# Column-normalised attention and a top-1 mixture of experts on one core: each batch's mixing set beside the next batch's Gram matrix, sums moved from GpSimd to VectorE and TensorE, two float32 Gram matrices, twelve float32 expert blocks

## The chip, the core and the metric

The kernel runs on one core of a Trainium2 chip. Its engines work side by side, each through its own instructions in the order in which they were queued: TensorE (PE; its weight loads are PEld), VectorE (DVE), ScalarE (ACT), GpSimd (POOL) and SyncE (SP), which here only starts transfers. An engine whose next instruction has to wait starts nothing behind it. Transfers run on 16 DMA engines, started by SP (plain loads and stores) and by POOL (gathers and scatters with row numbers). The metric is device microseconds of one execution.

## The reference

```
qn = q / (norm(q, axis=1) + 1e-6);  kn = k / (norm(k, axis=1) + 1e-6)    # q, k, v: [4, 5056, 256]
s = kn.transpose(0, 2, 1) @ qn / tau;  a = softmax(s, -1)                # a: [4, 256, 256]
x = (v @ a).reshape(20224, 256)
logits = x @ w_gate;  e_idx = argmax(logits, 1);  probs = softmax(logits)
for e in range(8):                                                       # w1[e]: [256, 1024], w2[e]: [1024, 256]
    mask = e_idx == e
    out[mask] = probs[mask, e] * sigmoid(x[mask] @ w_output_gate[:, e]) * (relu(x[mask] @ w1[e]) @ w2[e])
```

## The kernel before

For each of the four batches there are three kinds of work, and a fourth for the whole.

**Gram** (`gram`, L244). 20 steps, each of two tiles of 128 rows of q and k (two transfers of 256 KB). TensorE adds k-transposed times q into `s_ps` (L282). Batch 0 multiplies in float32; batches 1 to 3 split q and k into a float32r high part (ACT, L265) and the remainder (DVE, L267) and multiply three times. The squares (ACT, L275) are summed into two accumulators `acc`, one on POOL and one on DVE (L277). At the end TensorE sums them over the rows (L294, L297), and some twenty small steps turn them into norms, softmax and the split matrix `ah`, `al` (L305 to L351).

**Mix** (`mix`, L356). 5 groups of 1024 rows of v: transposes (L378), a split (L382, L384), x and its logits in three multiplications (`x_ps`, L389 to L391), x stored to `xd` (L398). `route` (L404) finds each row's expert and place, and POOL scatters 8 x 128 entries into the table `tab` (L474).

**Checkpoints and blocks.** At a checkpoint (`checkpoint`, L601) the number of full blocks of 256 rows that each expert surely has is turned into a list of jobs (`table`, L491), after a mark is read back from `tab` (L486). There is one after group 2 of batch 0 and one at each batch's end. A block gathers row numbers (L686) and rows (L702), gets its expert's weights (L672), and goes through the two layers: `h_ps` (L790 to L792), ReLU and split (L794, L795), `y_ps` (L647 to L649), scaling (L653) and a scatter to the output (L655). The first 8 blocks are *cold*: float32 with the weights as they come (L772, L645), fetched anew for each block. The others are *hot*: float16 with high and low parts, three multiplications, and no fetch when the block two places earlier had the same expert. 72 full and 21 half blocks.

**Weight preparation** (`prep`, L212), 16 steps of 1 MB, two buffers. Load (L218, L222); sum of squares (ACT, L228); its sum over partitions by `partition_all_reduce` on POOL (L230); a power of two (DVE, L200 to L207); high part (ACT, L233); low part (DVE, L234); two stores to `wsc` (L238). Hot blocks need all 16.

The functions are generators. `_drive` (L28) emits from several side by side in proportion to their lengths, and a list scheduler then sets each engine's order from the dependencies, its own idea of durations and hints: `attend` (L862) ran Gram and mix of a batch one after the other with high priority, and `issue_after` held single transfers behind others.

Of the kernel before, what the change touches and what calls it, by code (L numbers as in the profile page):

```python
# [21 lines left out]
P = 128  # L22
# [18 lines left out]
def tile_colnorm_attention_then_top1_moe(  # L41
# [35 lines left out]
    CKS = [(0, 2), (0, NG - 1)] + [(b, NG - 1) for b in range(1, B)]  # L77
# [29 lines left out]
    WHOLE = (0,)  # L107
    NCOLD = 8
    GATE = 1
    HOLD = 3  # L110
    PGATE = 4
# [6 lines left out]
    first = []  # L118
# [6 lines left out]
    v_loads = [[] for _ in range(B)]  # L125
# [59 lines left out]
    def pow2(m, kk, scale, inv):  # L185
        """scale = 2^(kk - floor(log2 m)), inv = 1 / scale; both exact."""
# [10 lines left out]
    def root2(ss, kk, scale, inv):  # L197
        """scale: the power of two for which 2^(kk - 2) < scale * sqrt(ss) < 2^kk; inv = 1 / scale."""
# [13 lines left out]
    def prep():  # L212
        for e in range(E):
            for half in range(2):
                raw = big.tile([P, HW1], F32, tag="raw", name=f"raw{e}_{half}")
                with tc.issue_after(v_loads[0][PGATE]):
# [11 lines left out]
                nc.scalar.activation(hi, raw, AF.Square, accum_out=ss)  # L228
                tot = sm.tile([P, 1], F32, tag="wtot", name="wtot")
                nc.gpsimd.partition_all_reduce(tot, ss, P, bass_isa.ReduceOp.add)  # L230
# [11 lines left out]
    a_of = {}  # L242

    def gram(b):  # L244
        s_ps = ps_s.tile([P, CC, C], F32, tag="s", name=f"s_ps{b}")
        accs = [one.tile([P, 2, 2, C], F32, tag=f"acc{i}", name=f"acc{b}_{i}") for i in range(2)]
        nstep = NT // 2
        for st in range(nstep):
            t0 = 2 * st
            last = st == nstep - 1  # L250
            qk = ld.tile([P, 2, 2, C], F32, tag="qk", name=f"qk{b}_{st}", bufs=4)
            for i, src in enumerate((q, k)):
                main = src[b, :MAIN].rearrange("(p t) c -> p t c", p=P)
                nt = 1 if last else 2
                with tc.issue_after(v_loads[b - 1][GATE]) if b else nullcontext():
                    nc.sync.dma_start(qk[:, i, :nt, :], main[:, t0 : t0 + nt, :])
                    if last:
                        nc.sync.dma_start(qk[:REM, i, 1, :], src[b, MAIN:])
                if last and REM < P:
                    nc.gpsimd.memset(qk[REM:, i, 1, :], 0.0)  # L260
            if b in WHOLE:
                terms = [(qk, qk)]
            else:
                hi = wk.tile([P, 2, 2, C], F32R, tag="qkh", name=f"qkh{b}_{st}")
                nc.scalar.copy(hi, qk)  # L265
                lo = wk.tile([P, 2, 2, C], F32R, tag="qkl", name=f"qkl{b}_{st}")
                nc.vector.tensor_tensor(out=lo, in0=qk, in1=hi.bitcast(F32), op=ALU.subtract)  # L267
                terms = [(hi, hi), (hi, lo), (lo, hi)]
            on_pool = (st % 3 != 1) if b == 0 else (st % 2 == 0)
            acc = accs[int(on_pool)]  # L270
            if st < 2:
                nc.scalar.activation(acc, qk, AF.Square)
            else:
                sq = wk.tile([P, 2, 2, C], F32, tag="sq", name=f"sq{b}_{st}")
                nc.scalar.activation(sq, qk, AF.Square)  # L275
                eng = nc.gpsimd if on_pool else nc.vector
                eng.tensor_tensor(out=acc, in0=acc, in1=sq, op=ALU.add)  # L277
            for t in range(2):
                for c in range(CC):
                    cs = slice(c * P, (c + 1) * P)  # L280
                    for n, (kt, qt) in enumerate(terms):
                        nc.tensor.matmul(  # L282
                            s_ps[:, c, :], kt[:, 1, t, cs], qt[:, 0, t, :],
                            start=st == 0 and t == 0 and c == 0 and n == 0,
                            stop=last and t == 1 and n == len(terms) - 1,
                            skip_group_check=True,
                        )
            yield

        n_ps = ps_x.tile([P, 2, C], F32, tag="x", name=f"n_ps{b}")  # L290
        k_ps = ps_x.tile([P, 512], F32, tag="x", name=f"k_ps{b}")
        parts = [(i, t) for i in range(2) for t in range(2)]
        for n, (i, t) in enumerate(parts):
            nc.tensor.matmul(n_ps[:, 0, :], onesf, accs[i][:, 0, t, :], start=n == 0, stop=n == 3)  # L294
        for c in range(CC):
            for n, (i, t) in enumerate(parts):
                nc.tensor.matmul(  # L297
                    k_ps[:, c : c + 1], accs[i][:, 1, t, c * P : (c + 1) * P], onesf[:, 0:1],
                    start=n == 0, stop=n == 3, skip_group_check=True,
                )  # L300
        rq = one.tile([P, C], F32, tag="rq", name=f"rq{b}")
        rk = sm.tile([P, CC], F32, tag="rk", name=f"rk{b}")
        for r, ss in ((rq, n_ps[:, 0, :]), (rk, k_ps[:, :CC])):
            root = one.tile(list(r.shape), F32, tag="root", name="root", bufs=2)
            nc.scalar.activation(root, ss, AF.Sqrt)  # L305
            nc.vector.tensor_scalar(out=root, in0=root, scalar1=1e-30, scalar2=None, op0=ALU.max)
            nc.vector.reciprocal(r, root)
            nc.vector.tensor_tensor(out=r, in0=ss, in1=r, op=ALU.mult)
            nc.vector.tensor_tensor(out=r, in0=r, in1=root, op=ALU.add)
            nc.vector.tensor_scalar(out=r, in0=r, scalar1=0.5, scalar2=1e-6, op0=ALU.mult, op1=ALU.add)  # L310
        nc.vector.tensor_scalar(out=rk, in0=rk, scalar1=tau_b, scalar2=None, op0=ALU.mult)
        nc.vector.reciprocal(rq, rq)
        nc.vector.reciprocal(rk, rk)
# [14 lines left out]
        for c in range(CC):  # L328
            nc.vector.tensor_scalar(out=s[:, c, :], in0=s[:, c, :], scalar1=se[:, c : c + 1], scalar2=None, op0=ALU.mult)
# [18 lines left out]
        nc.scalar.copy(ah[:, :, :C], s)  # L348
        nc.scalar.copy(ah[:, :, C:], awv)
        nc.vector.tensor_tensor(out=al[:, :, :C], in0=s, in1=ah[:, :, :C].bitcast(F32), op=ALU.subtract)  # L350
        nc.vector.tensor_tensor(out=al[:, :, C:], in0=awv, in1=ah[:, :, C:].bitcast(F32), op=ALU.subtract)  # L351
# [4 lines left out]
    def mix(b):  # L356
        ah, al = a_of[b]
        for g in range(NG):
# [5 lines left out]
            for i in range(R // 2):  # L364
                if i % 2 == 0:
                    vt = ld.tile([P, 4, C], F32, tag="v", name=f"v{b}_{g}_{i}", bufs=3)
                    if np_ < P:
                        nc.gpsimd.memset(vt[np_ // 32 * 32 :], 0.0)
# [122 lines left out]
    def table(nm, mf, unit, Q, g0, step, nc_=0, wait=None):  # L491
# [81 lines left out]
        if nc_:  # L573
            nc.vector.tensor_copy(wi[:, :nc_], tmp[:, :nc_])
# [340 lines left out]
```

## Time and profile before

| | us |
|---|---|
| median of 3 runs | 1704.95 |
| lowest and highest run | 1701.8, 1712.46 |
| span of the profiled execution | 1590.9 |
| median less span | 114.05 |

The span runs from the first to the last instruction; what an execution takes around it the profile does not show. In a row of the timeline stand the start, the duration, the engine, the line, what is written from what, and in brackets the idle time before it and what ended that. "issue" in that place is time in which the engine waited for nothing that the profile shows. Lines such as L230 are those of the kernel before.

### The profile page before, as it was taken

The page shows a single profiled execution, that of the slowest core. Times are in us where ns is not written, and L with a number is a line of the kernel's source. Part 1 is how long each engine was busy: PE and PEld are TensorE (multiplying, and loading weights), DVE is VectorE, ACT ScalarE, POOL GpSimd, SP SyncE. Part 2 cuts the span into 40 slices and gives each one's busy share as a digit, 9 for nine tenths or more (in the row PEclk, how much of TensorE's full clock was granted, in tenths as well). Part 3 has the DMA queues.
Part 4 walks back from the last instruction along what each step waited for, and adds up shares of the span by engine and source line. Part 5 has one row for each costly group of instructions (what it writes and reads, how often), then busy time and mean ns, then how long its engine had stood idle before and what let it go on. Part 6 is the DMA issues. An engine that isn't in the chain of part 4 may idle for free. (4 is left out here: it accounts for less than half of the span.)

```text
span 1590.9 us, 28639 instructions
## 1 busy us (share of the span) xinstructions
PE 1320.8 (83%) x10982; PEld 1193.9 (75%) x10982; DVE 741.7 (47%) x1982; ACT 632.1 (40%) x1143; POOL 937.9 (59%) x860
## 2 busy tenths in 40 slices
PE   7585465576689578977999899999898999999998
PEld 6485455565679477876988788888787899889997
DVE  2674453341234467436456443443443454445543
ACT  3584453353355446433443232323232333333332
POOL 6344545454546457656567756556565677777774
PEclk9697768698789789998999999999999999999999
DMA  8388776464889477451433111111112535231120
GB/s 298 116 287 212 128 198 215 142 206 113 235 266 294 140 261 201 138 122 31 109 119 71 55 41 48 48 41 48 48 43 68 193 122 171 83 98 48 49 95 21
DMA packets 117565, 207.59 MB, mean 130 GB/s; under 512 B 40812, under 2 KB 70774, under 8 KB 111796
## 3 DMA queue, kind: packets, MB, share of 16 engines
q1 hardware_dynamic: 66420, 116.43, 26.0%
q0 software_dynamic: 51008, 89.33, 17.8%
q8 instruction: 86, 1.41, 0.4%
q14 instruction: 51, 0.42, 0.1%
HBM read 295.76 MB, written 60.59 MB: 224 GB/s over the span
## 5 line engine op out<-in xcount | busy, mean ns | idle before, releaser
L790 PE MATMUL h_ps<-xt,wbuf 128*128 128x256 f16 (+1 forms) x1360 | 343.4, 262 | 42.1 <-DVE hb L795 27.5
L794 ACT ACTIVATE hb<-h_ps 128x512 f16<-128x512 f32 (+1 forms) x340 | 185.1, 545 | 485.7 <-PE h_ps L792 485.4
L791 PE MATMUL h_ps<-xt,wbuf 128*128 128x256 f16 (+1 forms) x1360 | 343.7, 262 | 0.0
L792 PE MATMUL h_ps<-xt,wbuf 128*128 128x256 f16 (+1 forms) x1360 | 343.5, 262 | 0.0
L647 PE MATMUL y_ps<-wbuf,hb 128*128 128x256 f16 x1192 | 326.6, 274 | 2.6 <-DMA wbuf<-wsc,tb_wif 1.5
L649 PE MATMUL y_ps<-wbuf,hb 128*128 128x256 f16 x1192 | 326.4, 274 | 0.0
L648 PE MATMUL y_ps<-wbuf,hb 128*128 128x256 f16 x1192 | 326.4, 274 | 0.0
L795 DVE SCALAR_TENSOR_TENSOR hb<-h_ps,hb 128x512 f16<-128x512 f32 (+1 forms) x340 | 209.2, 620 | 166.3 <-ACT hb L794 163.2
L474 POOL DMA_INDIRECT tab<-r_ig,r_si x160 | 188.6, 1179 | 78.9 <-issue 39.1
L702 POOL DMA_INDIRECT xg<-xd,b_ig x165 | 176.4, 1069 | 94.3 <-issue 43.0
L655 POOL DMA_INDIRECT out_dram<-yo,b_ig x165 | 169.8, 1029 | 57.4 <-issue 36.8
L277 POOL TENSOR_TENSOR acc<-acc,sq 128x1024 f32<-128x1024 f32 x39 | 94.3, 2418 | 138.7 <-issue 70.5
L791 PEld LDWEIGHTS <-wbuf 128*128 128x128 f16 x1360 | 134.4, 99 | 39.7 <-issue 25.7
L672 POOL DMA_INDIRECT wbuf<-wsc,tb_wif x128 | 130.0, 1015 | 57.9 <-issue 26.4
L790 PEld LDWEIGHTS <-wbuf 128*128 128x128 f16 x1360 | 134.3, 99 | 36.3 <-DMA wbuf<-wsc,tb_wif 13.6
L728 DVE TENSOR_REDUCE b_mx<-xg 128x2 f32<-128x512 f32 (+1 forms) x85 | 52.7, 619 | 233.5 <-DMA xg<-xd,b_ig 233.5
L792 PEld LDWEIGHTS <-wbuf 128*128 128x128 f16 x1360 | 134.3, 99 | 13.2
L275 ACT ACTIVATE sq<-qk 128x1024 f32<-128x1024 f32 x72 | 75.8, 1060 | 144.6 <-POOL acc L277 94.2
L686 POOL DMA_INDIRECT b_ig<-tab,tb_gif x72 | 75.8, 1053 | 97.1 <-DMA out_dram<-yo,b_ig 69.1
L647 PEld LDWEIGHTS <-hb 128*128 128x128 f16 x1192 | 117.2, 98 | 15.4 <-DMA wbuf<-wsc,tb_wif 1.7
L648 PEld LDWEIGHTS <-hb 128*128 128x128 f16 x1192 | 117.3, 98 | 14.8 <-issue 1.3
L649 PEld LDWEIGHTS <-hb 128*128 128x128 f16 x1192 | 117.1, 98 | 14.3
(188 smaller groups left out, 2559.1 us busy)
## 6 DMA issues: line engine op xcount, KB each, us to landing
qk<-in_q_dram SPq DMA_DIRECT2D x76, 256.0 KB, 5.4
qk<-in_k_dram SPq DMA_DIRECT2D x76, 256.0 KB, 5.3
v<-in_v_dram SPq DMA_DIRECT2D x32, 512.0 KB, 7.5
raw<-in_moe_w_dram SPq DMA_DIRECT2D x16, 1024.0 KB, 13.4
xd<-st SPq DMA_DIRECT2D x16, 1024.0 KB, 8.3
wsc<-whi SPq DMA_DIRECT2D x16, 512.0 KB, 7.1
wsc<-raw SPq DMA_DIRECT2D x16, 512.0 KB, 9.4
v<-in_v_dram SPq DMA_DIRECT2D x8, 480.0 KB, 7.4
```

What stands on the lines that cost most here:

```text
L474: ins = nc.gpsimd.indirect_dma_start(out=tab[:, :], out_offset=bass.IndirectOffsetOnAxis(ap=si[:np_, t : t + 1], axis=0), in_=ig[:np_, t, ...
L647: nc.tensor.matmul(y_ps[:, t, :], hb[:, 0, f, tsl], w2s[:, 0, f, :], start=st, stop=False, **kw)
L648: nc.tensor.matmul(y_ps[:, t, :], hb[:, 0, f, tsl], w2s[:, 1, f, :], start=False, stop=False, **kw)
L649: nc.tensor.matmul(y_ps[:, t, :], hb[:, 1, f, tsl], w2s[:, 0, f, :], start=False, stop=fin, **kw)
L655: ins = nc.gpsimd.indirect_dma_start(out=out[:, :], out_offset=bass.IndirectOffsetOnAxis(ap=job["ig"][:, t, 0:1], axis=0), in_=yo[:, t, :] ...
L672: nc.gpsimd.indirect_dma_start(out=dst.bitcast(F32) if cold else dst, out_offset=None, in_=wraw[half] if cold else wsc[half][:, :], in_off ...
L702: ins = nc.gpsimd.indirect_dma_start(out=xg[:, g % XGB, t, :], out_offset=None, in_=xd[:lim, :], in_offset=bass.IndirectOffsetOnAxis(ap=jb ...
L790: nc.tensor.matmul(hp, w1s[:, 0, c, fs], xh, start=fi == 0 and c == 0, stop=False, **kw)
L791: nc.tensor.matmul(hp, w1s[:, 0, c, fs], xl, start=False, stop=False, **kw)
L792: nc.tensor.matmul(hp, w1s[:, 1, c, fs], xh, start=False, stop=fin, **kw)
L794: nc.scalar.activation(hh, h_ps[:, :, :w], AF.Relu)
L795: nc.vector.scalar_tensor_tensor(out=hb[:, 1, 2 * fp : 2 * fp + 2, :w], in0=h_ps[:, :, :w], scalar=0.0, in1=hh, op0=ALU.max, op1=ALU.subtract,
```

## The change

The emission: batch b's mix now runs beside batch b+1's Gram; with batch 1 also the weight preparation; blocks from batch 1 on. `attend`, its priority and most hints are gone, and the checkpoint within batch 0 too, so that the first list comes after the whole of batch 0.

```diff
-    for b in range(B):
-        par = [(mix(b) if b == 0 else attend(b), (NG * (R // 2 + 1) + (NT // 2 + 1) * (b > 0)) / FAST)]
-        n = sum(q for (cb, cg), q in quotas.items() if cb < b or (cb == b and cg < NG - 1)) - LAG - nout
...
+    for b in range(B):
+        par = [(mix(b), NG * (R // 2 + 1))]
+        if b < B - 1:
+            par.append((gram(b + 1), NT // 2 + 1))
+        n = sum(q for (cb, cg), q in quotas.items() if cb < b) - LAG - nout
+        if b == 1:
+            par.append((preps, 2 * E + 1))
+        if n > 0:
+            par.append((some(n * FC // 2), n * FC // 2))
...
-    CKS = [(0, 2), (0, NG - 1)] + [(b, NG - 1) for b in range(1, B)]
+    CKS = [(b, NG - 1) for b in range(B)]
...
-    WHOLE = (0,)
-    NCOLD = 8
+    TS = 4
+    WHOLE = (0, 1)
+    NCOLD = 12
```

The sums: the weights' sum over partitions becomes a TensorE product with ones; all squares are added on DVE into one `acc`; a Gram's sums are one column each for q and k, their roots are taken on [128, 4], and the q norms are spread by a product with a diagonal matrix. Three instructions that scaled or split `s` become part of the split.

```diff
+                w_ps = ps_x.tile([P, 512], F32, tag="x", name="w_ps")
+                nc.tensor.matmul(w_ps[:, 0:1], onesf, ss, start=True, stop=True)
                 tot = sm.tile([P, 1], F32, tag="wtot", name="wtot")
-                nc.gpsimd.partition_all_reduce(tot, ss, P, bass_isa.ReduceOp.add)
+                nc.vector.tensor_copy(tot, w_ps[:, 0:1])
...
-                eng = nc.gpsimd if on_pool else nc.vector
-                eng.tensor_tensor(out=acc, in0=acc, in1=sq, op=ALU.add)
+                    nc.vector.tensor_tensor(out=acc, in0=acc, in1=sq, op=ALU.add)
...
-            nc.tensor.matmul(n_ps[:, 0, :], onesf, accs[i][:, 0, t, :], start=n == 0, stop=n == 3)
+        for i in range(2):
+            for c in range(CC):
+                for t in range(2):
+                    nc.tensor.matmul(
+                        k_ps[:, i * CC + c : i * CC + c + 1], acc[:, i, t, c * P : (c + 1) * P], onesf[:, 0:1],
+                        start=t == 0, stop=t == 1, skip_group_check=True,
+                    )
...
+            nc.vector.tensor_scalar(out=dq[:, c, :], in0=ident, scalar1=r[:, c : c + 1], scalar2=None, op0=ALU.mult)
+        nc.tensor.matmul(n_ps[:, :C], onesf, dq.rearrange("p c m -> p (c m)"), start=True, stop=True)
```

q and k come in transfers of four tiles (512 KB each, three buffers in place of four half as large). Cold blocks, too, no longer fetch weights when the block two places earlier had the same expert. The rest of the diff follows from these.

What this does to each engine's order, at three places. POOL in the weight preparation of before: `ISA` rows load code, `wtot` is the sum over partitions, `acc` a Gram's sum, `tab` the scatter of routing.

```order
L230 ISA
L230 ISA wtot<-wss 128x1
L277 ISA
L277 TENSOR_TENSOR acc_1_3989<-acc_1_3989,sq_16_5448 128x1024
L702 DMA xg<-xd,b_ig 128x256 x2
L230 ISA
L230 ISA wtot<-wss 128x1
L672 DMA wbuf_160<-in_moe_w_dram,tb_wif_993 128x2048
```

The same sum now, on PE between a cold block's products (`h_ps`, `y_ps`) and mixing (`x_ps`):

```order
L760 MATMUL h_ps<-xt_1690,wbuf_160 128x256 x4
L635 MATMUL y_ps<-wbuf_161,hb_1651 128x256
L225 MATMUL w_ps<-wss,onesf 128x1
L388 MATMUL x_ps<-ah_1424,vh 128x272
L389 MATMUL x_ps<-al_1425,vh 128x272
```

The sum has left POOL, whose queue now holds transfers only, and PE waits for ACT's `wss` at that row.

PE early in the mixing of batch 0, before (`s_ps` is Gram 1 from split parts, `vt_ps` the transposes):

```order
L391 MATMUL x_ps<-ah_423,vl 128x272
L389 MATMUL x_ps<-ah_423,vh 128x272
L282 MATMUL s_ps_1431<-qkh_5_1685 128x256
L390 MATMUL x_ps<-al_424,vh 128x272
L378 MATMUL vt_ps<-ident,v_0_2_486 128x128 x4
L282 MATMUL s_ps_1431<-qkl_5_1687,qkh_5_1685 128x256
L282 MATMUL s_ps_1431<-qkh_5_1685,qkl_5_1687 128x256
```

and now:

```order
L390 MATMUL x_ps<-ah_385,vl 128x272
L377 MATMUL vt_ps<-ident,v_0_2_469 128x128 x8
L276 MATMUL s_ps_427<-qk_4_815 128x256 x7
L276 MATMUL s_ps_427<-qk_5_885 128x256 x5
L388 MATMUL x_ps<-ah_385,vh 128x272
```

Gram 1 stays beside the mixing of batch 0, as float32 products straight from the loaded tile, with no ACT or DVE step ahead of them.

SP in the weight preparation, before (`raw` loads a weight, `wsc` stores one, `qk` and `v` feed Gram and mixing):

```order
L238 DMA wsc_98<-whi_0_1706 128x2048
L256 DMA qk_13_5182<-in_q_dram 128x512
L256 DMA qk_13_5182<-in_k_dram 128x512
L486 DMA mark<-tab 128x2
L238 DMA wsc_98<-raw_0_1704 128x2048
L238 DMA wsc_99<-whi_1_1793 128x2048
```

and now:

```order
L235 DMA wsc_98<-whi_0_1842 128x2048
L235 DMA wsc_98<-raw_0_1840 128x2048
L397 DMA xd<-st_0_1583 1024x1x256
L235 DMA wsc_99<-whi_1_2019 128x2048
L213 DMA raw_0_2130<-in_moe_w_dram 128x2x1024
L235 DMA wsc_99<-raw_1_2017 128x2048
L369 DMA v_3_0_2992<-in_v_dram 128x1024
```

The preparation, which before ran from the mixing of batch 0 to that of batch 2, now stands packed between the mark of batch 0 and the rest of Gram 3: two loads ahead, in Gram 0, the other 14 here, each queued behind stores of the step before.

More of the change, by code (lines that the diff above doesn't have):

```diff
@@ L245, in gram @@
         s_ps = ps_s.tile([P, CC, C], F32, tag="s", name=f"s_ps{b}")
[L246 to L247 removed]
+        acc = one.tile([P, 2, 2, C], F32, tag="acc", name=f"acc{b}")
+        nstep = NT // TS
         for st in range(nstep):
[L249 removed]
+            t0 = TS * st
             last = st == nstep - 1
[L251 removed]
+            qk = ld.tile([P, 2, TS, C], F32, tag="qk", name=f"qk{b}_{st}", bufs=3)
@@ L261, in gram @@
[L261 to L275, printed above, removed]
-                eng = nc.gpsimd if on_pool else nc.vector
[L277 to L287, printed above, removed]
@@ L301, in gram @@
-        rq = one.tile([P, C], F32, tag="rq", name=f"rq{b}")
[L302 to L310, printed above, removed]
@@ new lines, in gram @@
+            for t0 in range(0, TS, 2):
+                qp = qk[:, :, t0 : t0 + 2, :]
+                if st == 0 and t0 == 0:
+                    nc.scalar.activation(acc, qp, AF.Square)
+                else:
+                    sq = wk.tile([P, 2, 2, C], F32, tag="sq", name=f"sq{b}_{st}_{t0}")
+                    nc.scalar.activation(sq, qp, AF.Square)
+                    nc.vector.tensor_tensor(out=acc, in0=acc, in1=sq, op=ALU.add)
+                if b in WHOLE:
+                    terms = [(qp, qp)]
+                else:
+                    hi = wk.tile([P, 2, 2, C], F32R, tag="qkh", name=f"qkh{b}_{st}_{t0}")
+                    nc.scalar.copy(hi, qp)
+                    lo = wk.tile([P, 2, 2, C], F32R, tag="qkl", name=f"qkl{b}_{st}_{t0}")
+                    nc.vector.tensor_tensor(out=lo, in0=qp, in1=hi.bitcast(F32), op=ALU.subtract)
+                    terms = [(hi, hi), (hi, lo), (lo, hi)]
+                for t in range(2):
+                    for c in range(CC):
+                        for n, (kt, qt) in enumerate(terms):
+                            nc.tensor.matmul(
+                                s_ps[:, c, :], kt[:, 1, t, c * P : (c + 1) * P], qt[:, 0, t, :],
+                                start=st == 0 and t0 == 0 and t == 0 and c == 0 and n == 0,
+                                stop=last and t0 == TS - 2 and t == 1 and n == len(terms) - 1,
+                                skip_group_check=True,
+                            )
+                yield
@@ new lines, in gram @@
+        k_ps = ps_x.tile([P, 512], F32, tag="x", name=f"k_ps{b}")
+        for i in range(2):
+            for c in range(CC):
+                for t in range(2):
+                    nc.tensor.matmul(
+                        k_ps[:, i * CC + c : i * CC + c + 1], acc[:, i, t, c * P : (c + 1) * P], onesf[:, 0:1],
+                        start=t == 0, stop=t == 1, skip_group_check=True,
+                    )
+        ss = k_ps[:, : 2 * CC]
+        root = sm.tile([P, 2 * CC], F32, tag="root", name=f"root{b}")
@@ L314, in gram @@
+        nc.scalar.copy(rq, n_ps[:, :C])
         s = one.tile([P, CC, C], F32, tag="s_sb", name=f"s_sb{b}")
```

130 lines of the change are left out of this document (50 added, 80 removed).

## The prediction

> **What bounds the kernel now.** I read the page first, then the busy time by stage, then who waited for whom, then one stretch of the timeline.
>
> ```profile
> span 1590.9 us, 28639 instructions
> PE 1320.8 (83%) x10982; PEld 1193.9 (75%) x10982; DVE 741.7 (47%) x1982; ACT 632.1 (40%) x1143; POOL 937.9 (59%) x860
> PEclk9697768698789789998999999999999999999999
> ```
>
> PE is the busiest engine and is idle for 270 us; the windows say where. I cut them at the first mixing product (84), the first cold product (268) and the last one (563):
>
> ```profile
> 0.00:84.00 84.00, 56.25 (x263) 48.33 (x264) 38.07 (x54) 39.90 (x46) 39.89 (x37) 0.86 0.64 210
> 84.00:268.00 184.00, 112.22 (x799) 106.78 (x799) 99.95 (x250) 102.19 (x162) 93.79 (x69) 0.79 0.82 217
> 268.00:563.00 295.00, 203.23 (x1024) 185.68 (x1024) 106.57 (x252) 125.06 (x187) 144.02 (x120) 0.83 0.65 195
> 563.00:880.00 317.00, 273.50 (x2320) 247.11 (x2319) 174.32 (x534) 134.87 (x275) 202.62 (x184) 0.94 0.46 127
> 880.00:1230.00 350.00, 326.39 (x2915) 289.06 (x2915) 154.44 (x395) 107.66 (x204) 212.28 (x210) 0.98 0.16 48
> 1230.00:1591.00 361.00, 349.21 (x3669) 316.98 (x3667) 168.39 (x499) 122.45 (x272) 245.28 (x243) 1.00 0.30 98
> ```
>
> Columns: the stretch, its length, busy us of PE, PEld, DVE, ACT, POOL, granted clock, DMA share, GB/s. From 563 on PE works 949 of 1028 us (0.923). Before, it works 372 of 563, at a clock of 0.79 to 0.86, and no engine is full: DVE has 100 of 184. So engines wait for each other in turn:
>
> ```profile
> DVE r2e L200 <- POOL wtot L230: 126.6, 12, 28.8
> POOL acc L277 <- issue: 70.5, 7, 13.8
> POOL wtot L230 <- issue: 54.1, 7, 11.7
> 394.15 2.33 POOL L277 TENSOR_TENSOR acc<-acc,sq 128x1024 f32<-128x1024 f32 x1 [13.83 <-issue]
> 409.26 0.40 POOL L230 PARTITION_ALL_REDUCE wtot<-wss  x1 [7.72 <-issue]
> 409.69 0.15 DVE L200 TENSOR_SCALAR r2e<-wtot 128x1 int32<-128x1 int32 x1 [28.84 <-POOL wtot L230]
> 410.50 1.11 PE L378 MATMUL vt_ps<-ident,v 128*128 128x128 f32 x4 [18.73 <-DVE wsw L204]
> ```
>
> POOL alternates between its adder and its sum over partitions. At each change it is silent for about 8 to 10 us (54.1 / 7, 70.5 / 7) with nothing to wait for: the order has a code-loading row there. DVE stands behind it for 28.84 us, and PE, behind DVE, for 18.73. The reader sees one engine's code change stop three others. That is the first 563 us; what is lost there is lost for good, since PE is nearly full afterwards.
>
> **The change, part by part.** Prices, from stretches at full clock:
>
> ```profile
> 23.03 15.78 PE L282 MATMUL s_ps<-qk 128*128 128x256 f32 x72 [2.72 <-DMA qk<-in_k_dram]
> 84.18 0.29 PE L389 MATMUL x_ps<-ah,vh 128*128 128x272 f32 x1
> 85.06 0.29 PE L390 MATMUL x_ps<-al,vh 128*128 128x272 f32 x1
> 88.30 0.28 PE L282 MATMUL s_ps<-qkh,qkl 128*128 128x256 f32 x1
> 90.82 0.28 PE L282 MATMUL s_ps<-qkh,qkl 128*128 128x256 f32 x1
> 330.92 0.60 PE L378 MATMUL vt_ps<-ident,v 128*128 128x128 f32 x4
> 414.70 4.00 PE L772 MATMUL h_ps<-xt,wbuf 128*128 128x256 f32 x16
> 420.70 3.61 PE L645 MATMUL y_ps<-wbuf,hb 128*128 128x256 f32 x16
> 880.00:1230.00 350.00, 129.20 (x468) 46.19 (x467) 0.98 0.16 48
> ```
>
> A float32 Gram product is two passes of 0.219, 0.438 us; a float32r one 0.120 (21 steps from 88.30 to 90.82); a mixing product 0.126 (7 steps to 85.06); a transpose 0.15. A cold block is 32 passes of 0.25 and 32 of 0.225 and four transposes, 15.8 us. The last row is L790 alone, 16 to a block: 29.25 hot blocks in 350 us, so 11.97 us each, of them 11.16 busy.
>
> Gram 1 in float32: 80 x 0.438 - 240 x 0.120 = +6.3 us of PE; it takes 20 copies from ACT and 20 subtractions from DVE. Four blocks turned cold: 4 x (15.8 - 11.2) = +18.5. All adds on DVE: it is about half busy in every stage, so I cost them at nothing; without that cover the 39 that POOL had would cost 39 x 1.2 = 47. Bigger transfers of q and k, 80 issues fewer on SP: nothing; a first tile lands a little later, and two weights (2.1 MB) are now queued on SP within Gram 0. The 16 products `w_ps` have one column each and cost PE nothing by themselves. The weights that cold blocks no longer fetch are at most 16 of 24 MB; PE does not wait for them in the rows above, so they count only as room for other transfers. No checkpoint within batch 0: the first list comes only after its last group, which the stages below contain.
>
> *To the first mixing product, 84 to 76.* The tail of Gram 0:
>
> ```profile
> 56.40 2.08 PE L294 MATMUL n_ps<-acc,onesf 128*128 128x256 f32 x4 [6.83 <-DVE acc L277]
> 60.83 2.56 PE L297 MATMUL k_ps<-onesf,acc 128*128 128x1 f32 x12
> 67.36 0.15 DVE L307 RECIPROCAL rk<-root 128x2 f32<-128x2 f32 x1
> 72.31 0.88 DVE L316 SCALAR_TENSOR_TENSOR s_sb<-s_ps,rk,rq 128x256 f32<-128x256 f32 x2
> ```
>
> From 56.40 to 72.31 it takes 15.9. Now: 16 passes (3.4), root (1.5), seven tiny steps (1.2), diagonal, product, copy (1.3), together 7.4. The rest to 84.18 stays.
>
> *Mixing 0 with Gram 1, to 162.* By the order PE has left 58 Gram products (25.4), 240 mixing products, 80 transposes and routing (30.2 + 12 + 2.5): 70 us, so 146 from below. By then 38 MB must have moved: at the 217 GB/s of the second window 176 us, the end from above. I take the middle, as SP's queue puts Gram 1's loads ahead of v and PE meets them in that order.
>
> *To the first cold product, 216.* Mark, table, gathers:
>
> ```profile
> L486 SPq DMA_DIRECT2D mark<-tab x5: 320/341/376, 205.4 to 877.1; - x5
> L772 PEld LDWEIGHTS h_ps<-xt,wbuf x256: 312/337/340, 268.1 to 526.1; 128*128 128x128 f32 x128
> L474 POOL DMA_INDIRECT tab<-r_ig,r_si x160 | 188.6, 1179 | 78.9 <-issue 39.1 <-DVE r_si L465 16.1 <-DVE root L306 5.1
> ```
>
> Before, from the mark at 205.4 to the product at 268.1, 62.7; less two code loads (7.7 + 10.1), plus eight scatters ahead of the mark (8 x 1.179, 9.4): 54. Bounds are 45, where those scatters lie beside the end of mixing, and 63. PE has Gram 2 and the first rows of mixing 1 to do meanwhile, some 31 us by the order, and then waits.
>
> *Cold stage, to 498.* PE work up to the last cold first layer, counted in the order: 241 us, so 477 at 0.923. But hot blocks need all prepared weights, of which 14 are left from about 207 on:
>
> ```profile
> L228 ACT ACTIVATE whi<-raw x16: 1892/1910/1948, 99.3 to 538.0; 128x2048 f16<-128x2048 f32 x16
> L233 ACT ACTIVATE whi<-raw,wsw 128x2048 f16<-128x2048 f32 x16 | 32.0, 2004 | 83.3 <-DVE invw L207 54.8 <-DVE wsw L204 28.5
> L234 DVE SCALAR_TENSOR_TENSOR raw<-raw,wsw,whi 128x2048 f16<-128x2048 f32 x16 | 37.5, 2348 | 6.3 <-ACT whi L233 6.1
> raw<-in_moe_w_dram SPq DMA_DIRECT2D x16, 1024.0 KB, 13.4
> wsc<-raw SPq DMA_DIRECT2D x16, 512.0 KB, 9.4
> ```
>
> Before, a step took 29.2 us (99.3 to 538.0 in 15), the end from above. From below: 13.4 + 1.9 + 2.0 + 2.35 + 9.4 and some 2 for the small ones, 31, with two buffers 15.5. The code loads were (54.1 + 70.5) / 16 = 7.8 of the 29.2; without them 21.4. I take 20: 207 + 14 x 20, the last store and the first fetch (11.5), 498. New here is that PE waits at `w_ps` for ACT, which waits for the load; behind it stand cold products and mixing.
>
> *The rest, 983.* 949 less four hot blocks (44.6), less what is further along at this point (24 mixing and 12 Gram products, 12 transposes: 6.2), plus 20 cold products still open (9): 907, at 0.923 983. Mixing 2 and 3 are spread over 37 hot blocks, which I cost at nothing: the same instructions stood in the third window from the end, denser, and there PE worked 273.5 of 317.
>
> Sum: 498 + 983 = 1481, against 1590.9. The median lies 114 us above the span; I keep that, and predict **1595 us**.
>
> [...] After the stall that ends at 367.5, PE was slow for a while:
>
> ```profile
> 367.90 0.41 PE L282 MATMUL s_ps<-qkh,qkl 128*128 128x256 f32 x1
> 369.82 0.41 PE L282 MATMUL s_ps<-qkh,qkl 128*128 128x256 f32 x1
> 370.03 5.36 PE L772 MATMUL h_ps<-xt,wbuf 128*128 128x256 f32 x16
> ```
>
> Nine steps of 0.213 for 0.120, and 5.36 for the 4.00 above: some 2.5 us lost. Were each of the 14 waits at `w_ps` that long, 35 us. [...]
>
> **Rivals.** (a) *Preparation quite hidden*: at 15.5 a step it ends by 436, PE decides, T = 465 to 477; 1565. For it: every POOL wait is gone. Against: SP issues a load behind the stores of the step before. (b) *The transfers bound*: 101 MB by the hand-over, 122 if cold blocks still fetch every weight; 122 at 217 GB/s is 562, so 1659. Against: 217 came at a share of 0.82, and hot blocks at 48 GB/s hardly fetch weights. (c) *Cold clock* at each `w_ps`: 1630. (d) *The preparation becomes serial* (slower): each load waits for the store two steps on in SP's queue, so that a step is the whole 31 and some 2 of queueing: 207 + 14 x 33 + 11.5 = 680, span 1663, 1777. It decides from 27.8 us a step (498 becomes 608, the old span). Against: before, with all its waits, 29.2. (e) *No gain*: steps near 28, 1705.
>
> **Chances.** Forecast 0.50 (1565 to 1630 by itself), (a) 0.15, (b) 0.12, (c) 0.08, (d) 0.09, (e) 0.06. About 1% is what a measurement can tell from no change. Faster: forecast, a, b, c, 0.85; within 1%: e, 0.06; slower: d, 0.09. The range, 1550 to 1665, takes in a, b and c and leaves out d and e.
>
> **What would show it.** No wait of DVE for POOL, no "issue" of some 8 us on POOL; first mixing product near 76, first cold near 216, first hot near 498; steps of L223 about 20 us apart; from there 983 us with PE at 0.92. Wrong if a step is over 27 us, if PE stands at `w_ps` for more than 5 us a time, or if PE falls under 0.88 while mixing lies among hot blocks.

## The result, and the profile after

| kernel | median us | runs | ratio to before, 95% interval |
|---|---|---|---|
| before | 1707.83 | 4 | |
| changed | 1663.92 | 4 | 0.9757 [0.9715, 0.9799] |

The change makes the kernel 2.4% faster; 6.5% were forecast. The profiled execution took 1664.9 us, with a span of 1663.2, so 1.7 us lie around the span and not 114. All spans known from now on lie as close to their own times (1.7 to 2.0 us less). The profile of before, 1590.9, therefore belongs to a faster execution than the runs listed beside it. The runs of the study, on five chips, show why: on one chip (A below) before takes 1597.4 us, on the other four (B) 1719.1 to 1721.1. The profile shown ahead of the prediction fits A, the runs beside it lie near B, and the changed kernel's profile is of the kind of B. Each of the five was seen at one time only, so A and B stand for a chip together with whatever else held at that time. Experiments are compared with before on their own chip.

The page of the changed kernel: span, busy time by engine, and the clock granted to TensorE in 40 slices.

```profile
span 1663.2 us, 27785 instructions
PE 1405.0 (84%) x10782; PEld 1226.7 (74%) x10782; DVE 725.2 (44%) x1939; ACT 620.7 (37%) x1131; POOL 816.7 (49%) x789
PEclk9898699979999999898997989899999889999889
```

The landmarks, from the rows by source line (count, durations in ns, first and last start): first mixing product, first cold product, first step of the preparation, first hot product.

```profile
L388 PE MATMUL x_ps<-ah,vh x320: 283/289/787, 84.9 to 1161.5; 128*128 128x272 f32 x160
L760 PE MATMUL h_ps<-xt,wbuf x384: 380/402/634, 236.4 to 504.4; 128*128 128x256 f32 x192
L223 ACT ACTIVATE whi<-raw x16: 1895/1910/1925, 23.3 to 447.1; 128x2048 f16<-128x2048 f32 x16
L778 PE MATMUL h_ps<-xt,wbuf x1296: 216/272/437, 532.7 to 1653.4; 128*128 128x256 f16 x138, 128*128 128x128 f16 x48
```

The windows cut at these landmarks, at the last mixing product (1162.1) and at the first half block (1216.6). Columns as in the prediction: stretch, length, busy us of PE, PEld, DVE, ACT, POOL, granted clock, DMA share, GB/s.

```profile
0.00:84.90 84.90, 60.76 (x265) 51.32 (x265) 43.14 (x69) 43.21 (x50) 5.07 (x20) 0.90 0.72 253
84.90:236.40 151.50, 104.22 (x703) 97.13 (x702) 86.04 (x216) 77.30 (x133) 70.31 (x58) 0.84 0.70 205
236.40:532.70 296.30, 266.13 (x1435) 249.86 (x1434) 123.65 (x306) 159.92 (x245) 141.06 (x121) 0.94 0.69 206
532.70:1162.10 629.40, 544.94 (x4462) 463.37 (x4462) 275.10 (x745) 208.22 (x410) 329.02 (x323) 0.91 0.22 65
1162.10:1216.60 54.50, 45.14 (x346) 34.64 (x345) 25.93 (x116) 13.03 (x27) 32.10 (x32) 0.87 0.29 85
1216.60:1663.20 446.60, 383.77 (x3581) 330.39 (x3579) 171.33 (x490) 119.02 (x267) 239.19 (x237) 0.91 0.23 75
```

Up to the first hot product PE idles 102 of 533 us; before, in the profile of A, it idled 201 of 578. After it PE has 974 of 1130 us (0.86), at a clock of 0.91; before, in the same profile, it had 943 of 1013 (0.93).

A measure for what follows, so that kernels with different numbers of cold blocks can be compared: **work** is the number of PE's products times their durations at full clock (hot 0.109 us, half as wide 0.056, cold 0.25 and 0.225, mixing 0.126, a Gram pass 0.219 or 0.12, everything else 0.15), and **loss** is the length of a stretch less the work in it. It is an estimate, worked out from the prices of the prediction and, for the hot products, from the steps between such rows in the profile of before. Loss counts standing and slow-clock time alike.

| kernel (chip) | to first hot: length, work, loss | from there: length, work, loss |
|---|---|---|
| before (A) | 572, 347, 226 | 1017, 947, 70 |
| before (B) | 576, 347, 230 | 1151, 947, 204 |
| changed (B) | 533, 426, 106 | 1131, 893, 237 |

On the same kind of chip the change takes 124 us of loss away ahead of the hot blocks, adds 25 of work, and adds 33 of loss behind them, in a stage that was expected to run as before.

### The profile page after: what moved, and what is told of

The parts are those of the page before. It is cut to its first block, busy times and chain, and to the rows that moved or that the text cites. A ratio compares the mean times of both kernels' runs of the same rounds, so it can differ in the third digit from the quotient of the medians.

```text
span 1663.2 us, 27785 instructions
## 1 busy us (share of the span) xinstructions
PE 1405.0 (84%) x10782; PEld 1226.7 (74%) x10782; DVE 725.2 (44%) x1939; ACT 620.7 (37%) x1131; POOL 816.7 (49%) x789
## 4 chain that ended last, share of the span: by engine, by line
PE 44%; issue 8%; DMA 2%; another core or an unknown queue 2%; DVE 2%; POOL 1%; ACT 1%; POOLq 0%; DVEq 0%; ACTq 0%
PE y_ps L639 7%; PE y_ps L637 7%; PE y_ps L638 6%; PE h_ps L780 6%; PE h_ps L778 6%; PE h_ps L779 6%; PE xt_ps L734 1%; PE x_ps L388 1%; PE x_ps L390 1%; PE x_ps L389 1%; DVE hb L783 1%; PE s_ps L276 1%; ACT hb L782 1%; PE vt_ps L377 1%
## 5 line engine op out<-in xcount | busy, mean ns | idle before, releaser
L783 DVE SCALAR_TENSOR_TENSOR hb<-h_ps,hb 128x512 f16<-128x512 f32 (+1 forms) x324 | 199.2, 620 | 447.1 <-ACT hb L782 360.2
L782 ACT ACTIVATE hb<-h_ps 128x512 f16<-128x512 f32 (+1 forms) x324 | 172.9, 542 | 538.4 <-PE h_ps L780 323.8
L778 PE MATMUL h_ps<-xt,wbuf 128*128 128x256 f16 (+1 forms) x1296 | 333.2, 266 | 45.1 <-DVE hb L783 34.4
L780 PE MATMUL h_ps<-xt,wbuf 128*128 128x256 f16 (+1 forms) x1296 | 334.1, 267 | 11.3 <-issue 10.8
L779 PE MATMUL h_ps<-xt,wbuf 128*128 128x256 f16 (+1 forms) x1296 | 333.8, 267 | 10.3 <-issue 10.0
L468 POOL DMA_INDIRECT tab<-r_ig,r_si x160 | 169.9, 1062 | 217.6 <-DVE r_si L464 132.9
L662 POOL DMA_INDIRECT wbuf<-wsc,tb_wif x120 | 120.8, 1007 | 182.7 <-PE h_ps L780 116.0
L779 PEld LDWEIGHTS <-wbuf 128*128 128x128 f16 x1296 | 130.4, 101 | 63.5 <-issue 50.2
L780 PEld LDWEIGHTS <-wbuf 128*128 128x128 f16 x1296 | 130.8, 101 | 29.7 <-issue 16.4
L778 PEld LDWEIGHTS <-wbuf 128*128 128x128 f16 x1296 | 130.6, 101 | 28.8 <-issue 15.1
L639 PEld LDWEIGHTS <-hb 128*128 128x128 f16 x1128 | 116.5, 103 | 32.1 <-issue 14.1
L264 DVE TENSOR_TENSOR acc<-acc,sq 128x1024 f32<-128x1024 f32 x76 | 93.0, 1223 | 55.5 <-ACT sq L263 46.7
L388 PE MATMUL x_ps<-ah,vh 128*128 128x272 f32 x320 | 101.6, 324 | 18.1 <-issue 10.1
L394 ACT COPY st<-x_ps 128x272 f32<-128x272 f32 x160 | 58.4, 388 | 149.5 <-remote 58.1
```

The lines of the kernel that those rows point to most:

```text
L468: ins = nc.gpsimd.indirect_dma_start(out=tab[:, :], out_offset=bass.IndirectOffsetOnAxis(ap=si[:np_, t : t + 1], axis=0), in_=ig[:np_, t, ...
L639: nc.tensor.matmul(y_ps[:, t, :], hb[:, 1, f, tsl], w2s[:, 0, f, :], start=False, stop=fin, **kw)
L662: nc.gpsimd.indirect_dma_start(out=dst.bitcast(F32) if cold else dst, out_offset=None, in_=wraw[half] if cold else wsc[half][:, :], in_off ...
L778: nc.tensor.matmul(hp, w1s[:, 0, c, fs], xh, start=fi == 0 and c == 0, stop=False, **kw)
L779: nc.tensor.matmul(hp, w1s[:, 0, c, fs], xl, start=False, stop=False, **kw)
L780: nc.tensor.matmul(hp, w1s[:, 1, c, fs], xh, start=False, stop=fin, **kw)
```

## The experiments

The theory at the start was the prediction's: POOL's code loads gone, the new order filling PE. ("Code load" is the author's name for POOL's idle time at a change between its adder and its sum, 5.8 to 13.8 us in the profile of before; the order has `ISA` rows there, but what POOL does in that time no trace shows.) Its rivals: the 114 us lie inside the span and belong to the execution; the product `w_ps` holds PE up; the order itself costs.

**1. Which chip, and where the 114 us lie.** Before, unchanged:

> The kernel before, unchanged, profiled once more. Theory 1 (the profiled execution of before was not like its timed ones): the span comes out at about 1703 us, 2 us under its own time, and the 112 us more than 1590.9 lie inside the span, above all after the last cold product, where PE was at 0.923 and is now nearer 0.85, with the clock at 0.90. Theory 2 (the 114 us lie around the span, as the prediction had it): the span is again about 1591 us beside a time of 1705 us.

Chip A: 1595.04 us in the median; the profiled execution took 1591.24, and 1589.5 of them are span. So no more than 1.7 us lie around the span, but the span was again the short one: both theories missed, and chips came into question.

> The kernel before, profiled once more, to lie beside the changed kernel on one chip. Where it takes about 1597 us: the profile known from before, few clusters after the first hot product. Where it takes 1705 to 1720 us (theory C, the stalls belong to the chip): clusters of 2 to 5 us at the blocks' borders in this kernel too, 100 us or more of them in the stage of hot blocks, clock 0.91 or less.

Chip B: 1728.9 us, span 1727.1. The windows of before on B, from the first hot product (576.1) on, then the same stretches in the profile of A; the counts show that the instructions are the same.

```profile
576.10:901.30 325.20, 271.88 (x2067) 234.09 (x2068) 150.06 (x425) 121.06 (x249) 177.58 (x165) 0.87 0.40 111
901.30:1298.20 396.90, 365.67 (x3191) 316.74 (x3189) 177.04 (x489) 114.88 (x224) 230.01 (x227) 0.96 0.16 47
1298.20:1727.00 428.80, 367.26 (x3602) 311.50 (x3599) 161.75 (x492) 118.67 (x269) 242.03 (x240) 0.99 0.25 81
```

```profile
578.10:852.50 274.40, 245.35 (x2068) 222.08 (x2069) 149.52 (x425) 121.41 (x249) 174.69 (x159) 0.95 0.47 131
852.50:1237.40 384.90, 356.31 (x3191) 315.41 (x3190) 175.21 (x490) 117.87 (x224) 236.63 (x233) 0.98 0.17 49
1237.40:1590.90 353.50, 341.81 (x3602) 310.36 (x3599) 165.54 (x492) 120.96 (x269) 241.58 (x240) 1.00 0.30 99
```

Up to the first hot product the chips agree (576.1 on B, 578.1 and 572.4 on A); behind it B takes 138 us more, 51 beside mixing, 12 with full blocks alone, 75 with full and half blocks in turn. That is where the 114 us are. Theory C holds as to the time; of its low clock it holds beside mixing only (0.87), as the last stretch, which loses most, ran at 0.99.

The changed kernel was run four more times, each time on a B chip, with ratios of 0.9699, 0.9687 and 0.9706 where timed, and spans of 1663.9 to 1674.1:

> The changed kernel, unchanged, on a chip on which before is timed in the same call. Theory C (the stalls of TensorE without a waiting partner in the profile after, a cluster of 3.6 to 5.3 us at every second block, belong to the chip of that execution, on which before took 1705 us): where before takes 1597 us the ratio of 0.976 holds, 1558 us, and the clusters are gone. Theory S (they belong to the changed order): they are there again, some 110 us of them after the first hot product, and the time is 1640 us or more.

> The changed kernel beside before on one chip. On a chip where before takes 1597 us, theory C gives a span near the 1481 us of the prediction's sum plus the 34 us by which the first hot product came late, 1515 us, and no clusters after it; theory S gives 1560 us or more with the clusters. On a chip where before takes 1705 to 1720 us: 1664 us again.

> The changed kernel on the chip of this call. Where before takes 1597 us: 1515 us by theory C (the prediction's span of 1481 and the 34 us by which the first hot product came late), 1558 us if the ratio of the other chip holds, 1640 us or more by theory S. Where before takes 1705 to 1720 us: 1665 us again.

> The changed kernel on the chip of this call. Where before takes 1597 us: 1515 to 1560 us by theory C, 1640 us or more by theory S. Where before takes 1705 to 1720 us: 1665 us again.

So theories C and S were not told apart by the changed kernel itself on chip A; that stays open. An indirect answer comes from the next run.

**2. The sums alone, the order alone** (both on A).

```diff
+                w_ps = ps_x.tile([P, 512], F32, tag="x", name="w_ps")
+                nc.tensor.matmul(w_ps[:, 0:1], onesf, ss, start=True, stop=True)
...
-                nc.gpsimd.partition_all_reduce(tot, ss, P, bass_isa.ReduceOp.add)
+                nc.vector.tensor_copy(tot, w_ps[:, 0:1])
...
-                eng = nc.gpsimd if on_pool else nc.vector
+                eng = nc.vector
```

> Before, with only the two POOL sums moved: the weights' sum over partitions as a TensorE product with ones, all squares added on VectorE (still into two accumulators). Order, checkpoints, cold blocks, transfers as before. Theory A (the gain of the change is POOL's code loading): no wait of VectorE for POOL, the first hot product earlier by 30 us or more, 1665 us. Theory B (the gain is the new order, and the code loads were hidden behind other waits): within 10 us of 1705 us.

1526.97 us, 0.9567 [0.9530, 0.9603]: more than theory A said.

> The changed kernel, with the two sums back on POOL (partition_all_reduce; two accumulators, every second or third add on POOL) and, to make room for the second accumulator, q and k in transfers of two tiles with five buffers. Theory A (the gain is POOL's code loading): 1700 us or more, and code loading of 8 to 10 us shows again as issue on POOL. Theory B (the gain is the new order): 1665 us.

1612.06 us, 1.0101 [1.0061, 1.0141], as theory A had it (1700 us or more of 1705), and POOL has its two functions back. In this order the scheduler put the first weight sums into Gram 0, where POOL's adds waited behind them (first mixing product at 141.8), and POOL changes between its two functions 26 times, for 16 in before. So its start says nothing on the order. Its hot stage does. From the first hot product on it has the changed kernel's order, but for transfers of q and k that are half as large (3 rows against the last 3 of the changed kernel above):

```profile
641.10:1191.30 550.20, 509.10 (x4492) 457.28 (x4489) 270.00 (x745) 208.59 (x410) 340.20 (x328) 0.98 0.27 77
1191.30:1236.80 45.50, 38.97 (x347) 33.92 (x345) 25.93 (x116) 13.12 (x27) 30.95 (x31) 0.97 0.32 87
1236.80:1609.50 372.70, 349.53 (x3581) 312.35 (x3578) 170.08 (x490) 122.22 (x267) 240.64 (x238) 0.99 0.29 92
```

968 us on A for what takes 1130 on B: loss 71 against 237, which speaks for theory C. Beside before on A (70), the new order loses nothing there.

**3. The product with ones.** On B, the sums alone, and the sums with the changed end of a Gram (column sums, roots on 128x4, diagonal product):

> The two sums alone once more, on the chip of this call. Where before takes 1597 us: 0.957 again. Where it takes 1705 to 1720 us: theory T2 (the changed end of a Gram gains 8 us): 0.983; theory T3 (it gains nothing): 0.978.

> The run with the two sums alone, and in addition the changed end of a Gram (one column each for q and k, roots on 128x4, a diagonal product, scaling as part of the split). The prediction priced that at 8 us for batch 0, where nothing stands beside it; for the other batches it lies beside other work. Theory P: 8 us less than the sums alone, 1519 us where before takes 1597 us. Rival: TensorE waits elsewhere in its place, same within 4 us.

0.9766 [0.9727, 0.9806] and 0.9785 [0.9714, 0.9856]: theory T3, and the end of a Gram gains nothing. (Beside the adder alone, below, it even costs 0.8%: 0.9343 against 0.9262.) Then the adder alone (one line: all squares on VectorE, `partition_all_reduce` stays):

> Before, with only the adder moved: all squares are added on VectorE, the weights' sum over partitions stays on POOL. Theory L (what cost was the change of code on POOL, one load for each alternation): no code loading remains after the first sum, VectorE waits for POOL 20 us in all at most, and it gains as much as both sums moved, 0.957 of before, or 10 us more, since TensorE no longer waits at the weights' product. Rival M (POOL's sum itself and its queue behind gathers cost): VectorE still waits 60 us or more for POOL, 0.98 of before.

1593.21 us, 0.9262 [0.9219, 0.9305]: theory L, and by more than it said. VectorE waits 11.8 us for POOL in all, where before on B it waited 115.8. It beats the changed kernel on the same chip by 4.5% (1667.89). What the code loads alone cost was not measured: the adder also took its own time away from POOL (39 adds of 2.42 us, 1.22 each on VectorE), and no run leaves the adder on POOL and moves the weights' sum only. In the longest wait that the prediction shows, 28.84 us, the two loads are 13.83 and 7.72 and the add between them 2.33. And the clean pair: the run of both sums and the Gram's end, with only the weights' sum put back on POOL:

```diff
-                w_ps = ps_x.tile([P, 512], F32, tag="x", name="w_ps")
-                nc.tensor.matmul(w_ps[:, 0:1], onesf, ss, start=True, stop=True)
...
-                nc.vector.tensor_copy(tot, w_ps[:, 0:1])
+                nc.gpsimd.partition_all_reduce(tot, ss, P, bass_isa.ReduceOp.add)
```

> The run of both sums and the changed end of a Gram (0.9785 of before), with one thing undone: the weights' sum over partitions is on POOL again, as in the run with the adder alone (0.926). Theory W (the product with ones puts a wait for the weights into TensorE's queue, 73 us in that run, and mixing and cold blocks stand behind it): 0.93 of before, no such wait, the first hot product some 35 us earlier. Rival T (the changed end of a Gram is what cost): 0.975 of before.

0.9343 [0.9309, 0.9377] against 0.9785: theory W, some 76 us of 1720; the first hot product comes at 428.6 for 471.0. (The two runs are on two B chips; on the chip of the second, the sums alone take 0.9766.) Rows of who waited for whom (total, times, longest), one from before on B, one from the run with both sums and the Gram's end, one from the adder alone:

```profile
DVE r2e L200 <- POOL wtot L230: 115.8, 12, 29.3
```

```profile
PE w_ps L230 <- ACT whi L228: 73.2, 8, 27.4
```

```profile
POOL wtot L230 <- ACT whi L228: 77.6, 7, 52.6
```

The same data is waited for each time. In the second row PE stands, and everything queued behind it; in the third only POOL stands, with the transfers in its queue, and its waits end with ACT: of the seven sums from 95 to 260 us none has idle time put down to "issue" ahead of it, where POOL runs one such function only. Two of them:

```profile
144.84 0.39 POOL L230 PARTITION_ALL_REDUCE wtot<-wss  x1 [3.73 <-ACT whi L228]
167.90 0.34 POOL L230 PARTITION_ALL_REDUCE wtot<-wss  x1
```

In the profile of before POOL changes between its two functions 16 times, to and fro, and is idle for 5.8 to 13.8 us ahead of each of the 16; of these waits 7 of the sum (7.7 us each) and 7 of the adder (10.1 us each) have no partner.

In the changed kernel, by contrast, the product costs little:

```profile
PE w_ps L225 <- ACT whi L223: 14.1, 3, 6.8
```

> The changed kernel with the weights' sum over partitions on POOL again; the squares stay on VectorE, so POOL has one code. TensorE waited only 14 us for the weights in the changed kernel. Theory W2 (that wait and what stands behind it): 15 to 25 us less than the changed kernel, 0.955 of before. Rival V (eight sums now stand ahead of batch 0's scatters in POOL's queue, and POOL waits there for the weights): the first cold product later by 50 us or more, slower than the changed kernel.

0.9725 [0.9693, 0.9757]: neither. The last step of the preparation then begins at 287 instead of 447, yet the first hot product comes at 514.6, and what is gained there is lost behind it (loss 260).

**4. The parts of the order.** The changed kernel with 8 cold blocks, and with Gram and mixing of a batch one after the other:

```diff
-    NCOLD = 12
+    NCOLD = 8
```

> The changed kernel with 8 cold blocks in place of 12. Theory P (each cold block costs 4.6 us more of TensorE than a hot one): 18 us less than the changed kernel. Theory Q (the hot blocks would only wait longer for the prepared weights): within 5 us of the changed kernel, with TensorE idle ahead of the first hot product.

0.9879 [0.9819, 0.9939], 28 us slower. Both theories fall: the first hot product came at 482, but PE waited 39 us at `w_ps` (14 in the changed kernel), and the loss ahead of it rose from 106 to 149; what the rest of these 43 us is stays open.

```diff
...
-        par = [(mix(b), NG * (R // 2 + 1))]
-        if b < B - 1:
-            par.append((gram(b + 1), NT // 2 + 1))
+        par = [(attend(b), NG * (R // 2 + 1) + (NT // 2 + 1) * (b > 0))]
```

Here `attend` is `gram(b)`, then `mix(b)`.

> The changed kernel with one part of its emission undone: Gram and mixing of a batch one after the other again, as before, not mixing beside the next Gram; without the priority, the holds and the early checkpoint of before; all else as changed. Theory O (mixing beside Gram fills TensorE): slower than the changed kernel by 20 us or more. Theory N (the sums alone gain, the order gives nothing): within 10 us of it.

0.9703 [0.9645, 0.9762], as the changed kernel, so theory N as to the time: 27 us more lost at the start, 27 fewer behind. Mixing stays spread over the hot blocks here too (its last product comes at 1189.5, in the run with the adder alone at 774.4), so it is not the pairing with the next Gram that spreads it. Last, the same question from the other side, on the adder alone: the changed emission added to it (the loop of the change, no priority, no holds of q and k), and 12 cold blocks added to it:

> The run with the adder alone (0.926 of before on a chip where before takes 1721 us), and in addition the changed emission: mixing of a batch beside the next Gram, the preparation beside both, without the priority and the holds of q's and k's transfers; 8 cold blocks, the early checkpoint, one float32 Gram and small transfers as before. Theory E (mixing spread over more hot blocks costs TensorE 30 us or more after the first hot product): 0.945 of before or more. Rival F (the cold blocks, the float32 Gram and the missing early list cost, not the order): 0.935 or less.

> The run with the adder alone, with 12 cold blocks in place of 8. By the prediction's price 4 x 4.6 = 18 us more of TensorE, 0.937 of before. Rival G (as in the changed kernel, where 8 in place of 12 cost 28 us: the cold blocks fill the time of the preparation): 0.926 or less.

0.9640 [0.9611, 0.9669] and 0.9296 [0.9250, 0.9341]. Theory E holds: the new emission, with the priority and the holds taken away, costs some 65 us on B (0.9262 to 0.9640 of 1720). Which of the three does it was not tested one by one. Twelve cold blocks cost 6 us, a third of their price and within the intervals: the 0.937 of the price lies outside, the 0.926 of rival G inside. The hot stages of the adder alone (from 435.3), then of the same with the new emission (from 441.1):

```profile
435.30:774.80 339.50, 287.51 (x2262) 251.19 (x2261) 164.93 (x477) 135.87 (x272) 176.34 (x171) 0.90 0.40 115
774.80:1154.10 379.30, 350.65 (x3090) 304.63 (x3088) 171.01 (x476) 111.42 (x217) 221.69 (x219) 0.97 0.17 48
1154.10:1583.60 429.50, 369.06 (x3602) 313.44 (x3599) 162.64 (x492) 118.72 (x269) 241.21 (x240) 0.98 0.25 81
```

```profile
441.10:1149.30 708.20, 623.38 (x5087) 533.04 (x5086) 315.83 (x863) 241.74 (x468) 380.50 (x372) 0.92 0.26 78
1149.30:1204.40 55.10, 45.56 (x348) 35.03 (x346) 25.86 (x116) 13.12 (x27) 31.36 (x31) 0.85 0.26 76
1204.40:1652.00 447.60, 382.96 (x3581) 328.23 (x3578) 170.11 (x490) 118.67 (x267) 240.40 (x238) 0.91 0.23 76
```

The second window of the first kernel is 31 full blocks alone, PE at 0.92 and the clock at 0.97. The new emission leaves 3 such blocks: mixing lies among the other 41, PE at 0.88, clock 0.92. The last stage, too, is 18 us longer, with no mixing left in it and nearly the same instructions, at a clock of 0.91 for 0.98; why is open.

All of it in the measure from above (work and loss to the first hot product, and from there):

| kernel (chip) | ratio | to first hot | from there |
|---|---|---|---|
| sums alone (A) | 0.9567 | 306, 152 | 993, 76 |
| order with POOL's sums (A) | 1.0101 | 428, 213 | 896, 71 |
| sums alone (B) | 0.9766 | 306, 153 | 993, 227 |
| sums, Gram's end (B) | 0.9785 | 309, 162 | 996, 217 |
| adder alone (B) | 0.9262 | 334, 101 | 960, 188 |
| adder, Gram's end (B) | 0.9343 | 329, 99 | 970, 202 |
| adder, 12 cold (B) | 0.9296 | 455, 103 | 858, 178 |
| adder, new emission (B) | 0.9640 | 324, 117 | 969, 241 |
| changed, sum on POOL (B) | 0.9725 | 420, 94 | 894, 260 |
| changed, 8 cold (B) | 0.9879 | 332, 149 | 967, 243 |
| changed, one after the other (B) | 0.9703 | 409, 133 | 911, 210 |

The start depends on the order and on the sums, and hardly on the chip (sums alone: 152 and 153). The hot stage depends on the chip, and on B on the order as well.

## Why the prediction was wrong

Forecast 1595, measured 1664. In the profiled execution, 1664.9, the 70 us are 34.7 up to the first hot product (532.7 for 498), 33.5 from there (1130.5 for 983 + 114), and 1.7 around the span. The 34.7 are 8.9 to the first mixing product, 11 less beside Gram 1, 22.5 more from there to the first cold product, and 14.3 in the cold stage. So the prediction failed on both sides of the first hot product. That 1664 still lies just inside the range, 1550 to 1665, is luck: its upper end came from the bound of the transfers, rival (b), which is not what happened.

**"The median lies 114 us above the span; I keep that."** This is the step that failed in the hot stage. Only 1.7 us lie around the span. The 114 us are what the hot stage takes longer on a B chip, and there they depend on the order that the change rewrites: 138 us for before in the one trace of it on B, 162 for the order of the changed kernel (1130.5 less 968.4). A difference between a profile and the times beside it was carried over as a constant; it should have been a term of the stage where it arises, or a width of the range.

**"Mixing 2 and 3 are spread over 37 hot blocks, which I cost at nothing."** True on the chip of the profile it was read from: loss 71 against 70, and the stage forecast at 983 us took 968 on A. (The 15 us are an error of the sum: its 949 of 1028 us count from 563, the last cold product. From the first hot product, 578.1, PE has 943 of 1013, and the same sum gives 968.) False on B, where the emission adds 53 us of loss to the hot stage (241 against 188), though some 20 of them lie in the last stage, where no mixing is left. The test named for it, PE under 0.88 while mixing lies among hot blocks, came true (545 of 629, 0.87), but before on B fails it as well (272 of 325, 0.84).

**First mixing product, 76 forecast, 84.9.** The tail of Gram 0 was priced as the sum of its steps. Gram 1 now stands among them on the same engines (timeline of the changed kernel):

```profile
58.72 1.22 DVE L264 TENSOR_TENSOR acc<-acc,sq 128x1024 f32<-128x1024 f32 x1
64.31 1.22 PE L310 MATMUL n_ps<-dq,onesf 128*128 128x256 f32 x2 [9.73 <-DVE dq L308]
66.90 7.12 PE L276 MATMUL s_ps<-qk 128*128 128x256 f32 x22 [1.37 <-DVE s_sb L315]
73.85 0.60 PE L330 MATMUL at_ps<-ident,s_sb 128*128 128x128 f32 x4
74.29 4.91 PE L276 MATMUL s_ps<-qk 128*128 128x256 f32 x22
79.04 0.96 PE L339 MATMUL aw_ps<-wgo,at 128*128 128x16 f32 x8
```

Adds of 1.22 us stand between the tiny steps, and twice 22 passes of Gram 1 ahead of the transposes and of `aw_ps`. The softmax was ready at 68.7 and waited 5 us for PE, `at` at 75.1 and waited 4: with these 9 us the step is explained. Without the new emission the changed end of a Gram gained nothing here either (78.8 with the adder alone, 78.7 with the end added).

**Mixing beside Gram 1, to 162**: the last product ended at 159.9, but the stage took 75 us for 86, which made good the late start; that the end agrees is luck. **First cold product, 216**: 236.4. Between them lie 76 us, not 54: routing of the last group and its scatters follow the last product, and the mark came at 196.4, 36.5 us behind that product; only the scatters had been priced, at 9.4.

**Cold stage, 498**: the wrong bound, and with the late first cold product the step that failed ahead of the hot blocks. The preparation was faster than forecast, 15.0 us a step (251.6 to 447.1 in 13) for 20; done by about 460, it was hidden, as in rival (a). The first hot block waited for its list. POOL had gathered row numbers for 12 blocks before, all of them cold; the 13th, the first hot one, comes from the list of batch 1, whose mark is read at 504.25 (timeline of the changed kernel):

```profile
504.25 0.33 SPq L480 DMA_DIRECT2D mark<-tab  x1
506.66 1.05 POOL L676 DMA_INDIRECT b_ig<-tab,tb_gif  x1 [7.16 <-DVE tb_pm L562]
524.83 0.47 PE L734 MATMUL xt_ps<-ident,xs 128*128 128x128 f32 x1 [6.85 <-DVE xs L728]
```

From this mark to the first hot product, 532.7, it takes 28.5 us, a term that the prediction has nowhere. PE's own work sets when the mark comes: from the first cold product to the mark PE is busy for 246 of 268 us, close to the 241 of 261 behind the prediction's 477, which it set aside for the preparation. In the run with the weights' sum on POOL the preparation is done by about 300, and the first hot product still follows the mark of batch 1 (484.9) by 29.7. And the hand-over was not the lever it was taken for: with the weights' sum on POOL, or with 8 cold blocks, hot blocks start earlier and the kernel is no faster.

**Right:** the waits for POOL and its code loads are gone (VectorE waits 2.0 us for POOL in all, before on B 115.8 for the sum alone); four cold blocks and Gram 1 add 25 us of work, counted at the prediction's own prices (24.8 forecast); all adds on VectorE (1.22 us each) cost nothing that shows: the run with them alone is the fastest on B, 0.9262. "PE waits at `w_ps`" was seen as new, and is small in the changed kernel (14.1 us, once 6.8); in the old order the product costs 76. **Rivals:** (b) falls, as DMA's share is 0.69 to 0.72 in the stages that move most, against 0.82 in a stage of before; (d) and (e) fall by the step of 15 us; (c) falls in size: at the three waits at `w_ps` that the trace shows (3.3, 6.8 and 4.0 us) the clock was granted at half for 6.8, 10.2 and 6.8 us, which by estimate lost half of these 23.9 us at most, 12 for its 35; most of the slow clock sits in the hot stage (0.91 over 1131 us).

By parts, on B: moving the adder is worth 7.4%, moving the weights' sum to TensorE takes back 5, the new emission costs 4 where it meets the adder alone. The parts do not simply add up: the changed kernel keeps 3, since under the new emission the product is harmless (0.9725 with the sum on POOL, 0.9706 without, on one chip). The version to keep is the old order with the adder on VectorE and the weights' sum on POOL: 0.9262 of before on B; it was not run on A.

## What to carry to other kernels

Compare a profile's span with the times beside it before anything else; where they differ by far more than in the runs here (1.7 to 2.0 us, against 114 at first), take them for different executions, and locate the difference by profiling the old kernel again; don't add it to the new one's sum. When two functions alternate on an engine and the trace shows it idle at each change, as POOL here (5.8 to 13.8 us, 16 times), moving one away can be enough (0.9262). The sum that stayed did less harm on POOL, where its waits held up transfers (0.9343 of before), than as a product on TensorE, the busiest engine, which waited 73.2 us for its input (0.9785). Work spread over a stage was free where that stage ran undisturbed (on A a loss of 71 us for 70) and not on B (241 for 188), so its price belongs into the range.

## What was not expected of the hardware

The chips: identical instructions took 353.5 us on one and 428.8 on another in the stage of full and half blocks. On B, PE slows down once in every pair of a full and a half block without a partner that the trace shows, from one product each 0.11 us to one each 0.6 to 1.5, here and there up to 2.7, for 3.6 to 5.3 us (changed kernel from 1361 us on, PE; start, duration, idle time before):

```profile
1491.18 0.27 PE L779 MATMUL h_ps<-xt,wbuf 128*128 128x256 f16 x1
1491.88 0.27 PE L780 MATMUL h_ps<-xt,wbuf 128*128 128x256 f16 x1 [0.44 <-issue]
1492.59 0.27 PE L637 MATMUL y_ps<-wbuf,hb 128*128 128x256 f16 x1 [0.44 <-issue]
1493.31 0.28 PE L638 MATMUL y_ps<-wbuf,hb 128*128 128x256 f16 x1 [0.45 <-issue]
```

ACT is held as well, for 6.96 us in this case: its ReLU of a group whose last product began at 1446.36 starts at 1451.11 in before on B:

```profile
1451.11 0.66 ACT L794 ACTIVATE hb<-h_ps 128x256 f16<-128x256 f32 x2 [6.96 <-remote]
```

Behind most such stretches of the changed kernel the trace has the clock granted at half for 3.4 or 6.8 us, 17 times from 1252 to 1631; in before on B that happens three times in the whole last stage (clock 0.99), which still takes 75 us longer. In the traces of the B chips more than a third of the semaphore records are missing (13,289 for 21,127 in before). They are missing where the time is lost: in the first 200 us before has 2541 on B and 2758 on A, from 800 us on 1080 to 1166 in each 200 us on B and 2321 to 2878 on A. That signals between engines come late there would fit all three; it is the author's guess, and no run tests it. A rival guess fits as well: that the recording itself cannot keep up and holds the engines. Every run on record has a span, so each was recorded, and none without a recording is there to tell. Nor is it known whether the chip or what shares it makes the difference.
